# Row sums of the last four heads in one pass behind the attention, other pairs for the accumulating DMAs, and one load on GpSimd's queue

## The chip, the cores and the metric

The kernel runs on one core of one Trainium2 chip, alone. The metric is the device time of one execution in microseconds (us); lower is better. The core has a matrix engine (TensorE, PE in the profile), a vector engine (VectorE, DVE), an activation engine (ScalarE, ACT), GpSimd (POOL) and SyncE (SP). Each runs its own instructions strictly in order and waits for the others by semaphores. In this kernel SP and POOL mostly issue DMA transfers; the transfers of both run on the same 16 DMA engines. SP's transfers are queue q1 in the profile, POOL's are queue q0.

## What is computed

A gated mix of a 32-head attention block and a product-key expert layer over 2048 tokens of width 1024, all in float32:

```python
def _A_ref(x, wqkv, wo):                       # 32 heads of 32, 2048 tokens
    qkv = (x @ wqkv).reshape(B, S, 3, H, Dh).transpose(2, 0, 3, 1, 4)
    q, k, v = qkv[0], qkv[1], qkv[2]
    p = _softmax(jnp.einsum("bhqd,bhkd->bhqk", q, k) * (Dh ** -0.5), axis=-1)
    o = jnp.einsum("bhqk,bhkd->bhqd", p, v)
    return o.transpose(0, 2, 1, 3).reshape(B, S, D) @ wo
...
g = _sigmoid((x * gate_w).sum(-1, keepdims=True))
return g * _A_ref(x, A_wqkv, A_wo) + (1 - g) * b      # b: the expert layer
```

What matters here is the denominator of the softmax. The kernel computes the unnormalised output of a head and, apart from it, the sum of the exponentials of each query (the row sum); the factor gate / row sum is multiplied in only when the heads' outputs enter the last product with `wo`.

## The kernel before

Three stages follow each other. The first (up to about 480 us, and overlapping work to about 634 us) projects queries, keys and values and evaluates the expert layer. The second is the attention, head by head. The third multiplies the heads' outputs by `wo` in eight chunks of 256 tokens.

**Attention.** A head has 16 key tiles `kt` of 128 keys. For each, TensorE computes four score blocks of 512 queries into a ring of seven PSUM banks (`scores`, L1292), ScalarE takes their exponential into an SBUF tile `P[h, kt]` of 128 keys x 2048 queries (L1301), and TensorE multiplies the tile with the values (`pv`, L1313). The tile is also needed for the row sum: VectorE adds tiles to an accumulator `ACC[h]` (`presum` and `add`, L1354; one addition is two instructions of 128x1024). To relieve VectorE, some tiles are first added in pairs by an accumulating DMA from GpSimd's queue (`accumulate`, L1343: `P[h, b] += P[h, a]`), and only the sum is added to `ACC[h]` (`add_pair`, `merge`). `pairs_of` names the pairs (b, a). A place of a `P` tile is used again once its readers are done; `p_tile` picks the place by an estimate, `until`.

**Row sums.** For heads 0 to 27 the 128 partitions of `ACC[h]` are then folded to 32 by accumulating DMAs (`fold`, L1371), written to DRAM (`store_rows`, `SED`), folded there (`fold_rows`), and read back four heads together as `rr` (`load_r`), where VectorE adds the last two rows, takes the reciprocal and multiplies by the gate (`norm_r`); the result `RD` is the table of factors. The last four heads go another way. Head 29's accumulator is merged into the lower half of head 28's (`merge_odd`, `fold_odd`), and TensorE sums heads 28 and 29 with one product by a matrix of ones (`head_sums`, `rowsum`, L1326), head 30 with another; both use a bank of the ring within head 31's scores, which ScalarE empties (L1397). Head 31 is summed behind the attention, into a bank of its own. Each result goes to DRAM (`SMD`) by `norm_sums`, is read back by `load_r(7)`, and ends in `RD`.

**Order.** The order of work is written out by hand. A step is one key tile of one head (`base = 16 h`); `at(step, f, ...)` puts work to a step, and the main loop emits scores, the products with the values, the work of the step, then the addition of its tile. An engine's queue has its instructions in the order in which they are emitted.

**The last stage.** Chunk n needs the heads' outputs `OC[n]` (tile V, DRAM tensor `od`), the factors `RB[n]` (read from `RD`, tensor `rd`, each row copied to 32 partitions by the DMA), and their product split in a high and a low part (`split_o`, `scale_o` L1625, `split` L100 and L101). Chunks 0 and 1 are plain products (`wo_mm`, L1572); chunks 2 to 7 use a Strassen scheme of seven products P1 to P7 (`Halves.product`, L155), with prepared sums of `wo` (T1 to T4, DRAM tensors t0 to t3) loaded late. `RB[0]` is the tile `rb0`, which also serves as the accumulator of every third head; `RB[1]` and `RB[3]` share the place P9. `load_chunk(n)` loads `OC[n]` and `RB[n]`. Every DMA of SP waits for the eighth before it, since eight semaphores go round.

Of the kernel before, what the change touches and what calls it, by code (L numbers as in the profile page):

```python
# [10 lines left out]
F32 = mybir.dt.float32  # L11
# [6 lines left out]
S = 2048  # L18
# [14 lines left out]
def gated_mha_peer_kernel(ctx, tc, xT, wqkv, wv, wo, wq, k12, ug, v, out):  # L33
# [36 lines left out]

    ones2 = const.tile([128, 32], F32, name="ones2")
    nc.vector.memset(ones2, 0.0)
    for i in range(2):
        nc.vector.memset(ones2[64 * i:64 * i + 64, 16 * i:16 * i + 16], 1.0)


    const.tile([128, 152], F32, name="fill")
    ctx.enter_context(tc.tile_pool(name="fillr", bufs=1, side="right")).tile([128, 120], F32, name="fillr")
# [1083 lines left out]
    def p_tile(h, kt):  # L1162


        k = h * NT + kt
        n = [places for places, k0 in PLACES if k >= k0][-1]
        free = [i for i in range(n) if i not in (8, 9) or k < H * NT - 8]
        if k >= H * NT - 6:
            free = [i for i in free if i in ((0, 3, 7) if k >= H * NT - 2 else (1, 2, 3, 4, 5, 6))]
        i = min(free, key=lambda i: until[i])  # L1170
        pairs = pairs_of(h)
        until[i] = k + (16 if kt in [b for b, _ in pairs] else 10 if kt in [a for _, a in pairs] else 5)
        pool, name = ((pools["right"], f"P{i}") if i < 4 else (pools["left"], f"P{i}") if i < 8 else
                      (wk, f"P{i}") if i < 10 else (keep, ("vhl", "wo_raw2", "wo_raw3")[i - 10]))
        P[h, kt] = pool.tile([128, S], F32, name=name, bufs=1)
        return P[h, kt]
# [145 lines left out]

    def rowsum(ps, *srcs, ones=ones):
        for src in srcs:
            for qc in range(NQ):
                yield nc.tensor.matmul(ps[32 * qc:32 * qc + 32, :], ones,  # L1326
                                       src[:, qc * 512:(qc + 1) * 512],
                                       start=(src is srcs[0]), stop=(src is srcs[-1]))

# [30 lines left out]

    def merge_odd(h):
        add(ACC[h][up], ACC[h][up], pair(h, -1)[up])
        add(ACC[h - 1][low], ACC[h][low], pair(h, -1)[low])

    def fold_odd(h):
        nc.gpsimd.dma_start(ACC[h - 1][low], ACC.pop(h)[up], accum_op=OP.add)

    def fold(h, n):  # L1370
# [9 lines left out]

    def head_sums(h, heads=1):
        i, = ring_banks(1)
        for ins in rowsum(ring[:, i, :], ACC.pop(h), ones={1: ones, 2: ones2}[heads]):
            on_ring(ins, i)
        on_ring(norm_sums(h, ring[:, i, :], heads), i)

# [6 lines left out]

    def norm_sums(h, ps, heads=1):
        g, j = divmod(h, 4)
        o = wk.tile([128, 512], F32, name="ssb")
        ins = nc.scalar.activation(o, ps, AF.Copy)  # L1397
        for i in range(heads):
            dma(SMD[g][j + i:j + i + 1, :].rearrange("o (q s) -> (o q) s", q=NQ), o[32 // heads * i::32, :])
        return ins  # L1400

# [27 lines left out]
    def load_rb(n, k0, k1, js=range(4), queue=nc.sync):  # L1429
        if k0 == 0 and js[0] == 0:  # L1430
# [10 lines left out]

    OH, OL, W0 = {}, {}, []

    def split_first(step):
        o = OC[0][:, 0, :]
        if step == 0:
            W0.append(zp.tile([128, 2, D], F32R, name="z1"))
            OH[0] = zp.tile([128, KC, W], F32R, name="z0")
            OL[0] = wk.tile([128, KC, W], F32R, name="acc")
            nc.vector.tensor_mul(o, o, RB[0][:, 0, :])  # L1450
        elif step == 1:
            nc.scalar.activation(W0[0][:, 0], raw_wo(0), AF.Copy)
        elif step == 2:
            nc.scalar.activation(OH[0][:, 0, :], o, AF.Copy)
        else:
            for lo, src, hi in ((W0[0][:, 1], raw_wo(0), W0[0][:, 0]),
                                (OL[0][:, 0, :], o, OH[0][:, 0, :])):
                nc.vector.tensor_tensor(out=lo, in0=src, in1=hi.bitcast(F32), op=OP.subtract)
# [6 lines left out]
    for h in range(H):  # L1465
# [6 lines left out]
        if h < H - 1:  # L1472
# [16 lines left out]
        if j == 3 and g + 1 < G:  # L1489
# [77 lines left out]
    def wo_mm(pa, n, kcs, first, last):  # L1567
        for kc in kcs:
            wh, wl = (W0[0][:, 0], W0[0][:, 1]) if n == kc == 0 else (woh[kc], wol[kc])
            for a, b, i in ((OH[n], wh, 0), (OH[n], wl, 1), (OL[n], wh, 2)):  # L1570
                for tt, half in pa:
                    nc.tensor.matmul(pa[tt, half], a[:, kc, tt * 128:(tt + 1) * 128],  # L1572
                                     b[:, half * 512:(half + 1) * 512],
# [86 lines left out]
    for kc in range(1, KC - 1):  # L1660
        split_hi(kc + 1)
        if kc == 1:
            norm_sums(H - 1, sm)
            load_r(G - 1)
            pso.close()
# [165 lines left out]
```

## Time and profile before

| | us |
|---|---|
| median of three runs | 1808.73 |
| lowest and highest of them | 1805.19, 1809.46 |
| the profiled execution, its own time | 1804.75 |
| its span, first to last instruction | 1803.0 |
| TensorE busy in the span | 1795.0 |
| VectorE busy | 1495.4 |
| ScalarE busy | 1217.9 |
| GpSimd busy | 275.4 |
| SP's DMA queue, share of 16 engines | 36.4% |
| GpSimd's DMA queue, share of 16 engines | 36.4% |

The profiled execution is 4.0 us shorter than the median and 0.4 us shorter than the lowest run. Times within the trace count from the span's start. In the rows of a timeline the columns are start, duration, engine, line, operation, output and inputs by tile names, the shape and the number of merged instructions; a bracket tells the idle time before it and what ended it. Rows on SPq are the sequencer of SP while it issues a transfer. A matrix product in float32 appears as two instructions.

### The profile page before, as it was taken

How to read it: one execution, taken by the hardware profiler on the slowest of the kernel's cores; microseconds unless marked ns; L12 is line 12 of the kernel's file. 1: busy time of each engine (PE TensorE's matmuls, PEld its weight loads, DVE VectorE, ACT ScalarE, POOL GpSimd, SP SyncE). 2: the span in 40 equal slices, each digit the busy share in tenths (PEclk: the TensorE clock that was granted, in tenths of full speed). 3: DMA queues.
4: the chain of work that ended last, by engine and by line, in shares of the span. 5: the costliest groups of instructions: out<-in, count | busy, mean ns of one | idle time of the engine just before them, and what ended most of it. 6: DMA issues, size and time to landing. Idle time of an engine off the chain costs nothing.

```text
span 1803.0 us, 27887 instructions
## 1 busy us (share of the span) xinstructions
PE 1795.0 (100%) x10567; PEld 1136.7 (63%) x10567; DVE 1495.4 (83%) x1671; ACT 1217.9 (68%) x1608; POOL 275.4 (15%) x341
## 2 busy tenths in 40 slices
PE   9999999999999999999999999999999999999999
PEld 7877777788888855555554555555555545547787
DVE  7868776358987789999999999989989989895684
ACT  4434321211233399999999999999999999993221
POOL 0222000026401201111111111111111121111000
PEclk9999999999999999999999999999999999999999
DMA  6888888823238688899899999998999999977961
GB/s 237 242 284 249 276 264 288 269 79 107 83 119 283 229 197 170 179 182 204 174 206 195 195 205 191 193 196 192 201 221 197 202 220 193 201 161 204 280 179 66
DMA packets 132529, 361.14 MB, mean 200 GB/s; under 512 B 18516, under 2 KB 58596, under 8 KB 106968
## 3 DMA queue, kind: packets, MB, share of 16 engines
q0 software_dynamic: 22192, 132.79, 36.4%
q1 hardware_dynamic: 90040, 190.61, 36.4%
q10 hardware_dynamic: 20160, 35.92, 6.9%
q8 instruction: 84, 1.38, 0.3%
q14 instruction: 53, 0.43, 0.1%
HBM read 176.25 MB, written 86.09 MB: 146 GB/s over the span
## 4 chain that ended last, share of the span: by engine, by line
PE 96%; DMA 3%; SPq 1%; ACT 0%; DVE 0%; issue 0%; ACTq 0%; DVEq 0%
PE ring L1292 29%; PE o L1313 26%; PE bk L155 13%; PE bk L711 10%; PE pa L155 5%; PE bk L758 5%; PE bk L926 2%; PE bk L311 2%; PE bk L395 1%; PE bk L491 1%; SPq L82 1%; DMA wo_raw<-t1l 1%; DMA P<-rd 1%; PE pa L1579 1%; DMA smd<-ssb 0%; DMA woh<-t3h 0%
## 5 line engine op out<-in xcount | busy, mean ns | idle before, releaser
L1301 ACT ACTIVATE P<-ring 128x512 f32<-128x512 f32 (+3 forms) x982 | 807.3, 946 | 14.0 <-PE ring L1292 8.4
L1354 DVE TENSOR_TENSOR acc<-acc,P 128x1024 f32<-128x1024 f32 x418 | 482.2, 1218 | 26.5 <-ACT P L1301 26.5
L1313 PE MATMUL o<-P,V 128*32 128x512 f32 (+1 forms) x4040 | 414.4, 528 | 0.0
L1292 PE MATMUL ring<-Q,K 98*128 98x512 f32 x1024 | 269.0, 406 | 0.0
L1292 PE MATMUL ring<-z,z 98*128 98x512 f32 x1020 | 267.4, 406 | 0.1
L1292 PEld LDWEIGHTS ring<-Q,K 98*128 98x128 f32 x1024 | 182.8, 188 | 117.7 <-issue 37.0
L1292 PEld LDWEIGHTS ring<-z,z 98*128 98x128 f32 x1020 | 182.1, 188 | 114.7 <-ACT P L1301 38.9
L1313 PEld LDWEIGHTS o<-P,V 128*32 128x32 f32 x4040 | 111.5, 109 | 220.5 <-issue 200.5
L1354 DVE TENSOR_TENSOR rb<-rb,P 128x1024 f32<-128x1024 f32 (+1 forms) x188 | 217.4, 1218 | 11.6 <-ACT P L1301 11.6
L1343 POOL DMA_DIRECT2D P<-P x60 | 55.3, 922 | 427.5 <-PE o L1313 147.8
L240 ACT ACTIVATE hi<-bk 128x512 fp32r<-128x512 f32 x40 | 23.7, 595 | 118.5 <-PE bk L711 99.1
L1301 ACT ACTIVATE wo_raw<-ring 128x512 f32<-128x512 f32 (+3 forms) x110 | 99.4, 986 | 1.0 <-PE ring L1292 0.2
L711 PE MATMUL bk<-xh,e 128*128 128x512 f32 x384 | 94.2, 394 | 0.0
L711 PE MATMUL bk<-xl,e 128*128 128x512 f32 x384 | 92.3, 389 | 0.0
L711 PEld LDWEIGHTS bk<-xh,e 128*128 128x128 f32 x384 | 71.0, 188 | 22.0 <-issue 3.4
L253 DVE TENSOR_TENSOR lo<-bk,hi 128x512 fp32r<-128x512 f32 x40 | 27.6, 689 | 68.9 <-ACT hi L240 63.4
L711 PEld LDWEIGHTS bk<-xl,e 128*128 128x128 f32 x384 | 72.1, 188 | 15.0
L1301 ACT ACTIVATE vhl<-ring 128x512 f32<-128x512 f32 (+3 forms) x100 | 79.6, 881 | 0.9 <-PE ring L1292 0.6
L101 DVE TENSOR_TENSOR e<-wraw,e 128x512 fp32r<-128x512 f32 (+3 forms) x64 | 54.5, 859 | 26.6 <-ACT e L100 25.7
L100 ACT ACTIVATE e<-wraw 128x512 fp32r<-128x512 f32 (+3 forms) x64 | 44.7, 705 | 35.8 <-DMA wraw<-in_wqkv 20.2
L155 PE MATMUL bk<-xh,e 128*128 128x512 f32 x288 | 68.5, 393 | 0.0
L155 PE MATMUL pa<-woh,acc 128*128 128x512 f32 x192 | 62.6, 390 | 1.9 <-ACT acc L100 1.6
(311 smaller groups left out, 2445.0 us busy)
## 6 DMA issues: line engine op xcount, KB each, us to landing
P<-P POOLq DMA_DIRECT2D x60, 1024.0 KB, 10.5
wqt<-in_wq SPq DMA_DIRECT2D x26, 1024.0 KB
wraw<-in_wqkv SPq DMA_DIRECT2D x30, 512.0 KB
acc<-acc POOLq DMA_DIRECT2D x20, 512.0 KB, 5.5
qdh<-hi ACTq DMA_DIRECT2D x32, 256.0 KB
qdl<-lo ACTq DMA_DIRECT2D x32, 256.0 KB
kdh<-hi ACTq DMA_DIRECT2D x32, 256.0 KB
kdl<-lo ACTq DMA_DIRECT2D x32, 256.0 KB
```

Source lines behind the costliest of these rows:

```text
L100: nc.scalar.activation(hi, src, AF.Copy)
L101: (on or nc.vector).tensor_tensor(out=lo, in0=src, in1=hi.bitcast(F32), op=OP.subtract)
L155: nc.tensor.matmul(ps, self.a[a][i][:, k, :], self.b[b][j][k], start=(not first and k == 0 and i == j == 0), stop=(k == HC - 1 and i == 1))
L311: nc.tensor.matmul(ps[32 * quad:32 * quad + 32, :], kpad[:, quad % 2, i, :], t[:, quad, :], start=(i == 0), stop=(i == 3))
L711: nc.tensor.matmul(ps, t[:, kc // HC, a, kc % HC], x_at(b, n, kc), start=first, stop=last)
L758: nc.tensor.matmul(ps, x_at(a, t // 4, kc)[:, tok], b, start=first, stop=last)
L926: nc.tensor.matmul(p, x_at(a, t // 4, kc)[:, tok], b, start=first, stop=last)
L1292: on_ring(nc.tensor.matmul(ring[:, i, :], K[:98, kt * 128:(kt + 1) * 128], Q[:98, qc * 512:(qc + 1) * 512], start=True, stop=True), i)
L1301: on_ring(nc.scalar.activation(P[h, kt][:, q0 * 512:(q0 + m) * 512].rearrange("p (a m) -> p a m", a=m), ring[:, i:i + m, :], AF.Exp, scale ...
L1313: nc.tensor.matmul(O[h][32 * qc:32 * qc + 32, c0:c1], Vt[g][:, kt, 32 * j:32 * j + 32], p[:, qc * 512 + c0:qc * 512 + c1], start=(kt == 0) ...
L1343: nc.gpsimd.dma_start(P[h, b], P[h, a], accum_op=OP.add)
L1354: nc.vector.tensor_add(out[:, c], a[:, c], b[:, c])
```

## The change

Four things are changed together.

The row sums of heads 28 to 31 are all taken in one pass behind the attention. Heads 28 and 29 are now folded to 32 rows and stored like the others (into a new `SED[7]`); `merge_odd`, `fold_odd` and `head_sums` are gone. Head 30's accumulator is folded to 64 rows, and the stored 32 rows of heads 28 and 29 are read back into its other 64 partitions (`rows_back`, two transfers on GpSimd's queue). `rowsums` multiplies the two last tiles of head 31, its accumulator and this combined accumulator by columns of ones that put each head into 8 of 32 rows (`ones4`), into one bank. `norm_sums` writes four rows by four transfers.

The pairs become (0, 2), (3, 5), (6, 8) where they were (0, 2), (4, 6), (8, 10), and (0, 2), (6, 8) where they were (0, 2), (8, 10). Head 29 has two pairs in place of three. The estimate `until` of a pair's first tile is 18 steps in place of 16.

Since `rb0` is head 29's accumulator until its rows are stored, the factors of the first eight rows of chunk 0 go to a tile of their own (`load_first`, `zero`), those of 1 to 5 are loaded at step 11 of head 31, and `OL[0]` is made after the row sums.

The factors of chunk 3 (`load_rb(3)`) are loaded on GpSimd's queue, ahead of chunk 0's stores. Before, they followed `OC[3]` on SP's queue.

```diff
-    SED = [dram.tile([32, 4, S], F32, name=f"sed{g}") for g in range(G - 1)]
+    SED = [dram.tile([32, 4, S], F32, name=f"sed{g}") for g in range(G)]
...
+    ones4 = const.tile([128, 2, 32], F32, name="ones4")
+    nc.vector.memset(ones4, 0.0)
+    for rows, i, k in ((slice(64, 96), 0, 0), (slice(96, 128), 0, 1), (slice(0, 64), 0, 2), (slice(0, 128), 1, 3)):
+        nc.vector.memset(ones4[rows, i, 8 * k:8 * k + 8], 1.0)
...
-        if (h % 2 or (h % 4 and h < 17)) and h < 26 or h == H - 4:
-            return (0, 2), (8, 10)
-        return (0, 2), (4, 6), (8, 10)
+        if (h % 2 or (h % 4 and h < 17)) and h < 26 or h in (H - 4, H - 3):
+            return (0, 2), (6, 8)
+        return (0, 2), (3, 5), (6, 8)
...
-        until[i] = k + (16 if kt in [b for b, _ in pairs] else 10 if kt in [a for _, a in pairs] else 5)
+        until[i] = k + (18 if kt in [b for b, _ in pairs] else 10 if kt in [a for _, a in pairs] else 5)
...
+    def rowsums(ps, *srcs):
+        for k, (src, i) in enumerate(srcs):
             for qc in range(NQ):
+                nc.tensor.matmul(ps[32 * qc:32 * qc + 32, :], ones4[:, i], src[:, qc * 512:(qc + 1) * 512],
+                                 start=(k == 0), stop=(k == len(srcs) - 1))
...
+    def rows_back():
+        for j in range(2):
+            nc.gpsimd.dma_start(ACC[H - 2][64 + 32 * j:96 + 32 * j], SED[G - 1][:, j, :])
...
+    def norm_sums(ps):
         o = wk.tile([128, 512], F32, name="ssb")
+        nc.scalar.activation(o, ps, AF.Copy)
+        for j in range(4):
+            dma(SMD[G - 1][j:j + 1, :].rearrange("o (q s) -> (o q) s", q=NQ), o[8 * j::32, :])
...
+    def load_first():
+        zero["r"] = wk.tile([128, 512], F32, name="ssb")[:, :W]
+        for j in range(4):
+            dma(zero["r"][32 * j:32 * j + 32, :], RD[0, j:j + 1, :W].to_broadcast([32, W]))
...
-            at(base + NT + 6, merge_odd if h == H - 3 else merge, h)
-            if h == H - 2:
-                at(base + NT + 9, head_sums, h)
-            elif h == H - 3:
-                at(base + NT + 8, fold_odd, h)
-                at(base + NT + 15, head_sums, h - 1, 2)
-            else:
-                at(base + NT + 8, fold, h, 64)
-                if g + 1 < G:
-                    at(base + 2 * NT, fold, h, 32)
-                    at(base + 2 * NT + 8, store_rows, h)
+            at(base + NT + 6, merge, h)
+            at(base + NT + 8, fold, h, 64)
+            if h < H - 2:
+                at(base + 2 * NT, fold, h, 32)
+                at(base + 2 * NT + (5 if h == H - 3 else 8), store_rows, h)
...
-    at(30 * NT + 15, load_rb, 0, 0, KC - 2, range(2))
-    at((H - 1) * NT + 2, load_rb, 0, 0, KC - 2, range(2, 4))
-    at((H - 1) * NT + 13, load_rb, 0, KC - 2, KC - 1)
+    at(30 * NT + 15, load_first)
+    at((H - 1) * NT + 11, load_rb, 0, 1, KC - 2)
+    at((H - 1) * NT + 14, load_rb, 0, KC - 2, KC - 1)
+    at((H - 1) * NT + 14, rows_back)
...
-    list(rowsum(sm, *(P[H - 1, NT - i] for i in (1, 2)), ACC.pop(H - 1)))
+    rowsums(sm, *((P[H - 1, NT - i], 1) for i in (1, 2)), (ACC.pop(H - 1), 1), (ACC.pop(H - 2), 0))
+    OL[0] = wk.tile([128, KC, W], F32R, name="acc")
...
     split_o(1, HC, KC)
+    load_rb(3, 0, KC, queue=nc.gpsimd)
     load_at(2)
...
     plain_out(0, pa, nc.gpsimd)
-    load_chunk(3, 0, KC)
+    load_o(3, 0, KC)
```

On TensorE the order of scores and value products is the same as before; what is gone or moved are the products with ones. Before, the first of two such groups stood between the products with the values (tile V, bank `o`) and head 31's scores, in the ring:

```order
L1313 MATMUL o<-P_12566,V 32x512 x4
L1313 MATMUL o<-P_12573,V 32x256 x4
L1326 MATMUL ring<-acc,ones_111 32x512 x4
L1292 MATMUL ring<-Q_5229,K_5228 128x512 x9
L1313 MATMUL o<-P_12573,V 32x256 x4
```

Behind the attention, between the products of chunk 0's first eight rows (`pa`, inputs z and the low part) and those of its next, stood before:

```order
L1572 MATMUL pa_12927<-z_12763,acc 128x512
L1572 MATMUL pa_12928<-z_12763,acc 128x512
L1326 MATMUL o<-P_12878,ones 32x512 x4
L1326 MATMUL o<-P_12851,ones 32x512 x4
L1326 MATMUL o<-acc,ones 32x512 x4
L1572 MATMUL pa_12925<-woh_12909,z_12764 128x512
```

And stands in the change:

```order
L1559 MATMUL pa_12924<-z_12762,ssb 128x512
L1559 MATMUL pa_12925<-z_12762,ssb 128x512
L1326 MATMUL o<-P_12872,ones_112 32x512 x4
L1326 MATMUL o<-P_12847,ones_112 32x512 x4
L1326 MATMUL o<-acc,ones_112 32x512 x8
L1559 MATMUL pa_12922<-woh_12906,z_12763 128x512
```

Two groups of four products have left the ring, and one group of four has joined those behind the attention.

On GpSimd's queue, the end of the attention before (`acc<-rb` is `fold_odd`, P<-P are the pairs, `sed<-sed` folds in DRAM, `rr<-sed` the load of heads 24 to 27):

```order
L1366 DMA acc<-rb_5211 64x2048
L1343 DMA P_12443<-P_12480 128x2048
L1343 DMA P_12515<-P_12543 128x2048
L1378 DMA sed_94<-sed_94 16x1024
L82 DMA rr<-sed_94 128x2x64
L1343 DMA P_12655<-P_12688 128x2048
L1343 DMA P_12655<-P_12725 128x2048
```

And in the change (`rb<-rb` and `acc<-acc` are folds in SBUF, `sed_95` the new `SED[7]`):

```order
L1368 DMA sed_94<-sed_94 16x1024
L1361 DMA rb_5214<-rb_5214 32x2048
L82 DMA rr<-sed_94 128x2x64
L1365 DMA sed_95<-rb_5214 32x2048
L1342 DMA P_12653<-P_12687 128x2048
L1342 DMA P_12653<-P_12722 128x2048
L1361 DMA acc<-acc 64x2048
L1373 DMA acc<-sed_95 32x2048 x2
```

Head 30's fold and the two transfers of `rows_back` (L1373) stand behind the last pair of head 31; chunk 1's loads follow in both. In the same queue chunk 3's factors, four transfers of 32x8x256, now stand between chunk 1's loads and chunk 0's stores.

On VectorE, the first additions of head 30 before, with the numbers of the tiles (`rb0_5211` is head 29's accumulator; the 64x1024 rows are `merge_odd`):

```order
L1354 TENSOR_TENSOR acc_12461<-P1_12409,P8_12439 128x1024 x2
L1354 TENSOR_TENSOR acc_12461<-acc_12461,P7_12469 128x1024 x2
L1354 TENSOR_TENSOR rb0_5211<-rb0_5211,P0_12273 64x1024 x2
L1354 TENSOR_TENSOR acc_11984<-rb0_5211,P0_12273 64x1024 x2
L1354 TENSOR_TENSOR acc_12461<-acc_12461,P5_12504 128x1024 x2
L1354 TENSOR_TENSOR acc_12461<-acc_12461,P1_12518 128x1024 x2
```

And in the change:

```order
L1353 TENSOR_TENSOR acc_12497<-P9_12413,P0_12450 128x1024 x2
L1353 TENSOR_TENSOR rb0_5214<-rb0_5214,P1_12244 128x1024 x2
L1353 TENSOR_TENSOR acc_12497<-acc_12497,P2_12505 128x1024 x2
L1353 TENSOR_TENSOR acc_12497<-acc_12497,P9_12519 128x1024 x2
L1353 TENSOR_TENSOR acc_12497<-acc_12497,P1_12545 128x1024 x2
```

Before, the rows add tiles 1 and 3, tile 5, head 29's pair in two halves, then tiles 7 and 9. Now they add tiles 1 and 4, head 29's pair in one, then tiles 7, 9 and 10. From tile 9 on there are 21 additions (42 instructions) to the end of head 31 now; before, there were as many from tile 7 on.

More of the change, by code (lines that the diff above doesn't have):

```diff
@@ L69, in gated_mha_peer_kernel @@
     cbits = const.tile([1, 1], F32, name="cbits")
[L71 to L77, printed above, removed]
+    ones4 = const.tile([128, 2, 32], F32, name="ones4")
+    nc.vector.memset(ones4, 0.0)
+    for rows, i, k in ((slice(64, 96), 0, 0), (slice(96, 128), 0, 1), (slice(0, 64), 0, 2), (slice(0, 128), 1, 3)):
+        nc.vector.memset(ones4[rows, i, 8 * k:8 * k + 8], 1.0)
+    const.tile([128, 120], F32, name="fill")
     ctx.enter_context(tc.tile_pool(name="fillr", bufs=1, side="right")).tile([128, 120], F32, name="fillr")
@@ L1359, in gated_mha_peer_kernel @@
     up, low = slice(0, 64), slice(64, 128)
[L1361 to L1366, printed above, removed]
     def fold(h, n):
@@ L1379, in fold_rows @@
                              max_dma_last_dim=4 * S)
[L1381 to L1385, printed above, removed]
+    def rows_back():
+        for j in range(2):
+            nc.gpsimd.dma_start(ACC[H - 2][64 + 32 * j:96 + 32 * j], SED[G - 1][:, j, :])
     def finish(h):
@@ L1429, in load_rb @@
     def load_rb(n, k0, k1, js=range(4), queue=nc.sync):
-        if k0 == 0 and js[0] == 0:
+        if n not in RB:
             RB[n] = rb0 if n == 0 else wk.tile([128, KC, W], F32, name=f"P{8 + n % 2}", bufs=1)
@@ L1448, in split_first @@
             OH[0] = zp.tile([128, KC, W], F32R, name="z0")
-            OL[0] = wk.tile([128, KC, W], F32R, name="acc")
-            nc.vector.tensor_mul(o, o, RB[0][:, 0, :])
+            zero["lo"] = wk.tile([128, 512], F32R, name="ssb")[:, :W]
+            nc.vector.tensor_mul(o, o, zero["r"])
         elif step == 1:
@@ L1569, in wo_mm @@
             wh, wl = (W0[0][:, 0], W0[0][:, 1]) if n == kc == 0 else (woh[kc], wol[kc])
-            for a, b, i in ((OH[n], wh, 0), (OH[n], wl, 1), (OL[n], wh, 2)):
+            o_lo = zero["lo"] if n == kc == 0 else OL[n][:, kc]
+            for a, b, i in ((OH[n][:, kc], wh, 0), (OH[n][:, kc], wl, 1), (o_lo, wh, 2)):
                 for tt, half in pa:
-                    nc.tensor.matmul(pa[tt, half], a[:, kc, tt * 128:(tt + 1) * 128],
+                    nc.tensor.matmul(pa[tt, half], a[:, tt * 128:(tt + 1) * 128],
                                      b[:, half * 512:(half + 1) * 512],
@@ L1662, in gated_mha_peer_kernel @@
         if kc == 1:
-            norm_sums(H - 1, sm)
+            norm_sums(sm)
             load_r(G - 1)
```

15 lines of the change are left out of this document (2 added, 13 removed).

## Prediction

> **What bounds the kernel now.** I read the page's busy times first, then busy time by stretch, TensorE's waits in the last stage, and the timelines of the engines around the edits. A change of 0.3% (5.4 us) is about what a measurement of this kernel can tell from none.
>
> ```profile
> span 1803.0 us, 27887 instructions
> PE 1795.0 (100%) x10567; PEld 1136.7 (63%) x10567; DVE 1495.4 (83%) x1671; ACT 1217.9 (68%) x1608; POOL 275.4 (15%) x341
> ```
>
> TensorE is idle for 8.0 us of the span. By stretches (columns: start and end, length, busy time and instructions of PE, PEld, DVE, ACT, POOL, then TensorE's granted clock, DMA share, GB/s), the attention, the last stage and one head:
>
> ```profile
> 480.00:1618.00 1138.00, 1137.95 (x7535) 620.76 (x7537) 1042.89 (x996) 1031.72 (x1315) 172.49 (x227) 1.00 0.88 197
> 1618.00:1803.00 185.00, 179.32 (x816) 143.56 (x808) 115.07 (x165) 45.40 (x73) 9.52 (x17) 1.00 0.63 180
> 1036.91:1067.88 30.97, 30.97 (x217) 15.69 (x218) 29.68 (x27) 30.59 (x39) 4.77 (x8) 1.00 0.91 193
> ...
> PE pa L155 <- ACT acc L100: 1.6, 1, 1.6
> PE pa L155 <- DVE acc L101: 0.3, 1, 0.3
> ```
>
> The first two rows show TensorE without a gap in the attention and idle for 5.7 us behind it, of which the last two rows (TensorE's waits) are 1.86; the rest is the tail behind the last product. So this kernel has few microseconds to win: products that vanish, and 1.86. It has much to lose: in a head ScalarE is busy 30.59 and VectorE 29.68 of 30.97 us. One step, a key tile, is 30.97 / 16 = 1.94 us.
>
> **The products with ones.** TensorE around the two groups that are removed, and behind the attention:
>
> ```profile
> 1581.00 2.35 PE L1292 MATMUL ring<-z,z 98*128 98x512 f32 x9
> 1585.03 1.04 PE L1326 MATMUL ring<-acc,ones 128*32 128x512 f32 x8
> 1586.00 2.85 PE L1292 MATMUL ring<-Q,K 98*128 98x512 f32 x9
> 1606.83 1.04 PE L1326 MATMUL ring<-acc,ones 128*32 128x512 f32 x8
> ...
> 1625.74 1.04 PE L1326 MATMUL o<-acc,ones 128*32 128x512 f32 x8
> 1626.71 1.19 PE L1572 MATMUL pa<-woh,z 128*128 128x512 f32 x4
> ```
>
> A group costs 0.97 (1585.03 to 1586.00), two 1.94; the nine scores behind the first took 0.50 more than nine others (2.85 against 2.35). One group of 0.97 is added behind the attention, for the combined accumulator. So TensorE would reach its end 1.94 + 0.50 - 0.97 = 1.47 earlier, if nothing else held it.
>
> **VectorE holds it.** Its additions at the end of head 30 and in head 31:
>
> ```profile
> 1566.36 2.36 DVE L1354 TENSOR_TENSOR acc<-acc,P 128x1024 f32<-128x1024 f32 x2 [1.25 <-ACT P L1301]
> 1573.41 18.26 DVE L1354 TENSOR_TENSOR acc<-acc,P 128x1024 f32<-128x1024 f32 x16
> ...
> 1599.04 4.63 DVE L1354 TENSOR_TENSOR acc<-acc,P 128x1024 f32<-128x1024 f32 x4 [0.56 <-ACT P L1301]
> ...
> 1615.46 9.16 DVE L1354 TENSOR_TENSOR acc<-acc,P 128x1024 f32<-128x1024 f32 x8
> 1624.54 0.75 DVE L1599 TENSOR_TENSOR V<-V,rb 128x256 f32<-128x256 f32 x2
> ```
>
> From 1573.41 to the last addition, 1624.54, it does 21 additions (42 instructions) without a gap but 0.56: it is behind its tiles and would not feel TensorE running ahead. The last product with ones needs that addition: 1625.74 is 1.20 behind it. With the pairs (3, 5), (6, 8), head 30's unpaired tiles after its fifth step are 7 and 9 to 15, so the same 21 additions begin with tile 9. Tile 5 was ready at 1566.36; tile 9 is so four steps later, 1566.36 + 4 x 1.94 = 1574.1. The additions end at 1574.1 + 51.13 - 0.56 = 1624.7, 0.2 later than before. Behind them come head 31's accumulator and now one group more (0.97 each): chunk 0's products resume between 1626.7 and 1627.05, against 1626.71. The 1.47 is eaten by a wait that did not exist: **+0.3**, or -1.1 if the additions end 1.4 earlier.
>
> **The rows' way back.** The combined accumulator waits for two transfers on GpSimd's queue, behind the second pair of head 31 and the fold of head 30.
>
> ```profile
> 1609.13 0.85 POOL L1343 DMA_DIRECT2D P<-P  x1 [9.62 <-ACT z L1454]
> ...
> P<-P POOLq DMA_DIRECT2D x60, 1024.0 KB, 10.5
> acc<-acc POOLq DMA_DIRECT2D x20, 512.0 KB, 5.5
> ```
>
> Issue at 1609.13 + 0.85, landing within 10.5, some of the fold's 5.5 beside it, then some 5 to 6 for the read: it lands between 1622 and 1625, and is wanted at 1625.7. I take 0; if it is hidden no longer, each us is one of TensorE's, up to 5.
>
> **Four stores of row sums for one.** SP issues each in 0.53, and waits for the landing:
>
> ```profile
> 1586.76 1.06 SPq L82 DMA_DIRECT2D smd<-ssb  x2
> ...
> SPq L82 <- DMA smd<-ssb: 6.6, 1, 6.6
> ```
>
> Three more are 1.6 on the chain from row sums to factors. Chunk 0 and 1 run on 44 us of products (1626.71 to 1671.33) and only their last head groups need these factors; I take 0 here, with 1.6 as the other bound. Chunk 2 has about 1 to spare (next part), but its transfers are overtaken there by something larger.
>
> **Chunk 3's factors on the other queue.** Before, and the stall they cause:
>
> ```profile
> 1676.58 2.88 SPq L82 DMA_DIRECT2D P<-rd  x4
> ...
> 1688.75 2.36 DVE L1625 TENSOR_TENSOR V<-V,P 128x1024 f32<-128x1024 f32 x2 [7.78 <-DMA P<-rd]
> ...
> 1690.74 0.50 PE L155 MATMUL pa<-woh,acc 128*128 128x512 f32 x1 [1.57 <-ACT acc L100]
> ...
> DMA packets 1071, 1.04 MB, mean 115 GB/s; under 512 B 61, under 2 KB 1070, under 8 KB 1071
> q1 hardware_dynamic: 1071, 1.04, 88.7%
> ```
>
> Four issues from 1676.58 land just before 1688.75; VectorE waits 7.78 for them, and TensorE the 1.86 of above. The last two rows are the DMA view of 1678 to 1687: the load is 1 MB and holds 88.7% of all 16 engines for 9 us at only 115 GB/s, so 8.0 us of all engines. Moving it frees **1.86** there. Where does it go? Its place P9 is free once chunk 1's second half is multiplied:
>
> ```profile
> 1652.61 1.23 DVE L1640 TENSOR_TENSOR V<-V,P 128x1024 f32<-128x1024 f32 x1 [1.22 <-DMA P<-rd]
> 1652.80 10.58 SPq L82 DMA_DIRECT2D V<-od  x8
> ...
> 1664.34 1.23 DVE L1625 TENSOR_TENSOR V<-V,P 128x1024 f32<-128x1024 f32 x1 [4.89 <-DMA V<-od]
> 1668.43 1.23 DVE L1625 TENSOR_TENSOR V<-V,P 128x1024 f32<-128x1024 f32 x1 [2.87 <-DMA V<-od]
> 1669.58 0.69 DVE L101 TENSOR_TENSOR acc<-V,acc 128x512 fp32r<-128x512 f32 x1
> ...
> 1671.33 0.39 PE L155 MATMUL pa<-woh,acc 128*128 128x512 f32 x1
> ...
> 1650.00:1658.00 8.00, 8.00 (x37) 6.61 (x36) 3.31 (x4) 1.48 (x2) 0.00 (x0) 1.00 0.46 107
> 1658.00:1668.00 10.00, 10.00 (x46) 8.29 (x45) 2.52 (x3) 1.72 (x3) 2.15 (x4) 1.00 1.02 289
> ```
>
> P9 is free at 1652.61 + 1.23 = 1653.8, so the load is issued at about 1656 and moves from about 1658. There the DMA share is 1.02: these are the transfers of chunk 2 (`V<-od`, `P<-rd`) and the T sums, and VectorE waits for them already (4.89 and 2.87). The second half is multiplied at 1668.43, the low part of the first block is done at 1669.58 + 0.69 = 1670.27, and TensorE starts chunk 2 at 1671.33: 1.06 to spare. Eight us of engine time put into ten full ones must delay something by eight. If the queues take turns, SP's last transfer of chunk 2 ends about 8 later; I let 1 of it go to a share that falls to GpSimd only after 1668, so 7 later, and the stall is 7 - 1.06 = **6.0**. From below: with SP's transfers always first, the shift is some 0.5 and hidden. From above: if SP's queue stands while the load moves, the whole 9 and the 1.9 of start, less the spare, about 9.
>
> How two queues share can be seen once. From 1629 to 1636 GpSimd's queue reads factors the same way:
>
> ```profile
> q0 software_dynamic: 283, 0.82, 88.2%
> q1 hardware_dynamic: 19, 0.03, 1.0%
> ...
> 1634.69 0.33 SPq L82 DMA_DIRECT2D rr<-smd  x1
> ```
>
> SP's queue got 1.0% there, and the next SP issue came only at 1634.69, after the 6.6 of wait quoted above for a transfer of 8 KB. That leans away from "SP first" and toward a long delay; I stay between, since in that stretch SP had little to send.
>
> The Trainium skill ("Trainium Kernel Development and Optimization", Key Constraints) says that transfers issued from SP, ScalarE and GpSimd run on the same 16 DMA engines, and that several issuing engines save issue time alone. By that rule the move does not make 1 MB cheaper, only earlier, against full engines; the share of 1.02 agrees. "DMA: Bandwidth & Descriptors" (Queues, rings and completion order) says that an engine takes turns between queues packet by packet; by that rule alone the sum would be near its 6.0, but GpSimd's packets were larger in the rows above (0.82 MB in 283, some 2.9 KB, against 1 KB on SP's), which would give it more than half.
>
> **The pairs.** Each head has as many additions as before; in head 29 the pair that is gone costs one, and the merge that was done in two halves and is now one saves it. What could go wrong is a pair that is not there when its sum is added, or a `P` place that stays taken. A pair is issued four steps behind its first tile (steps 4, 7, 10), and the sums are added at steps 14, 18 and 22: 10, 11 and 12 steps later, 10 each before; 10 steps are 19.4 us, against the 10.5 of a pair. TensorE waits nowhere between 480 and 1618 now. I take 0; a missed place would cost some 2 per head (one step), over 31 heads up to 60, which I hold unlikely enough to leave it outside the range.
>
> **Sum.** +0.3 + 6.0 - 1.86 = +4.4 on the profiled execution's own time, 1804.75 (span 1803.0): 1809.2. The median of the runs is 1808.73, 3.98 above that execution; I carry the difference over to the median: 1813.2, 0.25% slower.
>
> **The rivals.**
> 1. *The move is hidden* (SP's transfers are not pushed back). For it: SP's transfers are issued from 1652.80, before the load. Against it: shares of 1.02 and 1.0%. Then 1.86 is won and VectorE takes 0.3 to 0.5 back: -1.4 to -1.6; with the 1.47 of TensorE's too, -3.3. Time 1805.4 to 1807.3: not slower, the other side of my forecast. It decides if the delay is below 1.06 + 1.86.
> 2. *SP's queue stands for the whole load.* For it: the 1.0%. Against it: P<-rd and V<-od of chunk 2 are partly through by 1658. Stall 9: +7.4, 1816.2. It decides from a stall of about 7 on.
> 3. *The rows come back late.* For it: only 1 to 3 us of room, in a queue of transfers of 10.5. Against it: little else moves then. Up to 5 on top of the forecast: +4.4 to +9.4, 1813 to 1818.
>
> **Chances.** Forecast 0.45 (its own range +2 to +6.5, 1810.7 to 1815.2), first rival 0.25, second 0.15, third 0.15. Range 1804 to 1820: the first rival's best with a spread of the median (1805.19 to 1809.46) to the third's worst. Faster by over 0.3% needs more than 5.4, which the removable work (1.47 + 1.86) does not hold: 0.06. Slower by over 0.3%: second rival 0.15, most of the third 0.10, the upper part of the forecast 0.19: 0.44. The rest, 0.50, is within.
>
> **What would show it.** At 1671 or some us later TensorE waits for chunk 2's first high or low part, with 5 to 7 of idle time, and DVE's scale_o(2) waits longer for V<-od; nothing near 1690. If TensorE starts chunk 2 without a wait, the first rival stands. The last addition of head 31 ends at 1624.5 to 1625.1, and TensorE waits there for it; a release by a DMA is the third rival. A head in the middle takes 30.97 still. A longer head would prove me wrong about the pairs, and the end of additions before 1623.5 about VectorE.

## The result and the profile after

| | before | after |
|---|---|---|
| median of six runs | 1806.45 us | 1813.49 us |
| lowest and highest | 1804.27 to 1809.46 | 1812.95 to 1816.45 |
| ratio of times, 95% interval | | 1.0040 (1.0027 to 1.0053) |
| span of the profiled execution | 1803.0 us | 1812.2 us |

The changed kernel is 0.40% slower, some 7 us. (The median of before was 1808.73 when the prediction was made; three more runs moved it.)

The page of the changed kernel (span, busy times), TensorE's waits from the end of the attention on, and busy time by stretch, with the columns of the prediction:

```profile
span 1812.2 us, 27968 instructions
...
PE 1798.1 (99%) x10559; PEld 1136.5 (63%) x10559; DVE 1495.0 (82%) x1673; ACT 1216.4 (67%) x1604; POOL 281.6 (16%) x351
```

```profile
PE pa L155 <- ACT acc L100: 4.7, 1, 4.7
PE o L1326 <- DMA acc<-sed: 2.1, 1, 2.1
PE pa L155 <- DVE acc L101: 0.2, 1, 0.2
```

```profile
480.00:1618.00 1138.00, 1137.89 (x7532) 621.22 (x7534) 1041.96 (x996) 1031.22 (x1312) 175.14 (x231) 1.00 0.88 196
...
1626.00:1630.00 4.00, 1.91 (x12) 0.21 (x12) 3.92 (x7) 1.67 (x3) 1.56 (x4) 1.00 0.95 300
1630.00:1634.00 4.00, 4.00 (x14) 3.16 (x11) 2.68 (x6) 3.81 (x6) 2.52 (x5) 0.57 1.01 330
1676.00:1681.00 5.00, 0.36 (x2) 0.00 (x0) 1.76 (x2) 0.58 (x1) 0.00 (x0) 1.00 1.04 399
1681.00:1684.00 3.00, 2.71 (x6) 1.70 (x7) 2.30 (x4) 0.68 (x2) 0.00 (x0) 0.55 1.02 428
```

The attention is as full as before. There are two waits behind it, one of 2.1 for the rows that come back, one of 4.9 at chunk 2; the 1.9 at chunk 3 is gone. And TensorE is busy for 3.1 us more, though it has eight matrix instructions fewer: behind each of the two waits its granted clock is near half (0.57, 0.55). TensorE's timeline shows the same; the last number of a row's head is the duration:

```profile
1582.32 2.35 PE L1292 MATMUL ring<-z,z 98*128 98x512 f32 x9
...
1624.88 2.07 PE L1326 MATMUL o<-acc,ones 128*32 128x512 f32 x8
1629.05 1.06 PE L1326 MATMUL o<-acc,ones 128*32 128x512 f32 x8 [2.09 <-DMA acc<-sed]
1630.05 2.05 PE L1559 MATMUL pa<-woh,z 128*128 128x512 f32 x4
1631.90 1.84 PE L1559 MATMUL pa<-wol,z 128*128 128x512 f32 x4
1633.57 1.08 PE L1559 MATMUL pa<-woh,acc 128*128 128x512 f32 x4
...
1675.29 1.07 PE L1559 MATMUL pa<-woh,acc 128*128 128x512 f32 x4
1681.10 0.64 PE L155 MATMUL pa<-woh,acc 128*128 128x512 f32 x1 [4.74 <-ACT acc L100]
...
1685.85 0.40 PE L155 MATMUL pa<-z,s 128*128 128x512 f32 x1
```

Against the rows of before, where the span's 9.2 us come from:

- 1.3 lie ahead of the edits to the last heads: the same scores of head 30 stand at 1582.32, 1581.00 before. 1.2 of it is there at the attention's first exponentials already (629.31 against 628.11), ahead of all pairs. Stage one ends earlier or later in each execution (in the profiles of the experiments below these exponentials stand between 0.5 earlier and 1.1 later than those of before), so I don't count this as an effect of the change.
- Chunk 0 goes on at 1630.05 in place of 1626.71, 3.34 later; without the 1.3 that is about the wait of 2.09.
- Its next eight instructions, 1630.05 to 1633.57, take 3.5 in place of 1.96 (1626.71 to 1628.67): 1.6.
- The wait at chunk 2 is 4.74 + 0.18 = 4.9, and the first product, 1681.10 to 1685.85, takes 4.75 in place of 2.72 (1671.33 to 1674.05), of which 1.85 are slow products.
- Chunk 3 saves its 1.86 and about 0.4 of slower products behind it.

1.3 + 2.1 + 1.6 + 4.9 + 1.85 - 2.3 = 9.45; the 0.25 over are not followed further.

### The profile page after: what moved, and what is told of

It is laid out like the page before. It is cut to its first block, busy times and chain, and to the rows that moved or that the text cites. A ratio compares the mean times of both kernels' runs of the same rounds, so it can differ in the third digit from the quotient of the medians.

```text
span 1812.2 us, 27968 instructions
## 1 busy us (share of the span) xinstructions
PE 1798.1 (99%) x10559; PEld 1136.5 (63%) x10559; DVE 1495.0 (82%) x1673; ACT 1216.4 (67%) x1604; POOL 281.6 (16%) x351
## 4 chain that ended last, share of the span: by engine, by line
PE 90%; DMA 4%; ACT 2%; DVE 1%; SPq 1%; issue 1%; POOL 0%; ACTq 0%; DVEq 0%; POOLq 0%
PE ring L1292 27%; PE o L1313 25%; PE bk L155 11%; PE bk L711 9%; PE pa L155 6%; PE bk L758 5%; PE bk L926 2%; PE bk L311 2%; PE bk L491 1%; ACT P L1301 1%; SPq L82 1%; DMA wraw<-in_wqkv 1%; DMA V<-od 1%; PE bk L395 1%; PE pa L1566 1%
## 5 line engine op out<-in xcount | busy, mean ns | idle before, releaser
L1353 DVE TENSOR_TENSOR acc<-acc,P 128x1024 f32<-128x1024 f32 x408 | 469.4, 1215 | 22.1 <-ACT P L1301 22.1
L1353 DVE TENSOR_TENSOR rb<-rb,P 128x1024 f32<-128x1024 f32 x186 | 214.3, 1215 | 5.6 <-ACT P L1301 5.6
L1342 POOL DMA_DIRECT2D P<-P x60 | 55.7, 928 | 362.9 <-PE o L1313 141.8
L1353 DVE TENSOR_TENSOR acc<-acc,wo_raw 128x1024 f32<-128x1024 f32 x60 | 70.1, 1216 | 1.8 <-ACT wo_raw L1301 1.8
```

The lines of the kernel that those rows point to most:

```text
L1342: nc.gpsimd.dma_start(P[h, b], P[h, a], accum_op=OP.add)
L1353: nc.vector.tensor_add(out[:, c], a[:, c], b[:, c])
```

## The experiments

All ratios are to the kernel before, measured beside each experiment, with 95% intervals. Its median differed from one time to another (1805.74 to 1806.65), so the rows are compared by their ratios.

| kernel | median us | ratio |
|---|---|---|
| the change | 1813.49 | 1.0040 (1.0027 to 1.0053) |
| e1_sp | 1810.53 | 1.0022 (1.0013 to 1.0032) |
| e2_fold | 1810.15 | 1.0022 (1.0012 to 1.0031) |
| e3_both | 1807.74 | 1.0007 (0.9997 to 1.0017) |
| e4_pool | 1810.28 | 1.0022 (1.0013 to 1.0032) |
| e5_fill | 1813.34 | 1.0040 (1.0026 to 1.0055) |
| e6_pairs | 1808.73 | 1.0012 (1.0002 to 1.0021) |
| e7_halves | 1804.38 | 0.9994 (0.9985 to 1.0004) |
| e8_step | 1805.62 | 0.9995 (0.9985 to 1.0004) |
| e9_clock | 1811.70 | 1.0033 (1.0021 to 1.0045) |
| e10_swap | 1805.96 | 1.0000 (0.9991 to 1.0009) |
| e11_pairs | 1808.91 | 1.0017 (1.0008 to 1.0026) |
| e12_store | 1804.65 | 0.9992 (0.9983 to 1.0001) |

**The load back on SP's queue (e1_sp).**

```diff
-    load_rb(3, 0, KC, queue=nc.gpsimd)
...
-    load_o(3, 0, KC)
+    load_chunk(3, 0, KC)
```

> The changed kernel with chunk 3's factors back on SP's queue, behind OC[3], as before. Theory (the collision): the 4.74 + 0.18 us that TensorE waits at 1681 and the slow products behind it (1681.10 to 1685.85 in place of 2.72, 2.0 us) go, and the wait of 1.9 at the start of chunk 3 comes back with 0.7 of slow products: 1813.5 - 6.9 + 2.6 = about 1809. Rival (the wait comes from the later row sums and the four stores, not from the load): TensorE still waits 4 to 5 us at the start of chunk 2, about 1813 to 1816.

Its waits of TensorE behind the attention, and one stretch:

```profile
PE o L1326 <- DMA acc<-sed: 3.4, 1, 3.4
PE pa L155 <- DVE acc L101: 0.3, 1, 0.3
```

```profile
1630.00:1634.00 4.00, 4.00 (x13) 2.86 (x10) 1.92 (x4) 3.49 (x6) 2.17 (x4) 0.50 0.90 232
```

The wait at chunk 2 is gone, so the load was its cause, not the later row sums or the four stores, which are all still there. Against the change the ratio fell by 0.18%, about 3.2 us, less than the 4.3 expected: the wait for the rows stands, here with 3.4 and a clock of 0.50 behind it. The wait of 1.9 at chunk 3, expected back, isn't (0.3 is left): TensorE comes there later, and starts chunk 3 at 1694.70 in place of 1690.74.

**The load alone moved, in the kernel before (e4_pool).** The opposite edit.

> The kernel before with only chunk 3's factors moved to GpSimd's queue, at the same place as in the change. Theory (the collision alone): TensorE waits 5 to 6 us at the start of chunk 2 and runs about 2 us of slow products, and the 1.9 + 0.7 at chunk 3 goes: 1806.5 + 4.5 to 5.5 = 1811 to 1812. Rival (the move costs something only with the later row sums of the change): within 1.5 of 1806.5, or faster by up to 2.6.

```profile
1676.30 0.80 PE L155 MATMUL pa<-woh,acc 128*128 128x512 f32 x1 [4.37 <-ACT acc L100]
```

The same wait at the same place, 4.37 and 0.62 more before the third product. The move alone makes the kernel before 3.6 us slower; expected were 4.5 to 5.5.

How the transfers met is in the changed kernel's own trace: GpSimd's issues and VectorE's wait, SP's issue of chunk 2's other input, and the two queues' packets, MB and share of the 16 engines from 1661 to 1670, with the time from issue to landing:

```profile
1658.85 2.34 POOL L82 DMA_DIRECT2D P<-rd  x4 [24.51 <-DVE V L1627]
...
1657.84 13.37 SPq L82 DMA_DIRECT2D V<-od  x8
...
1679.16 2.54 DVE L1612 TENSOR_TENSOR V<-V,P 128x1024 f32<-128x1024 f32 x2 [14.84 <-DMA V<-od]
```

```profile
q1 hardware_dynamic: 801, 0.76, 57.5%
q0 software_dynamic: 189, 0.66, 33.2%
...
P<-rd POOLq DMA_DIRECT2D x1, 256.0 KB, 15.5
```

VectorE waits 14.84 for SP's `V<-od`, whose issue stretches to 13.37 (10.58 before). SP's queue does not stand still: it has 57.5% against 33.2%, and the load takes 15.5 for a quarter.

**Head 30's fold ahead of head 31's second pair (e2_fold).**

```diff
-            at(base + b + 4, accumulate, h, b, a)
+            at(base + (9 if (h, a) == (H - 1, 6) else b + 4), accumulate, h, b, a)
```

> The changed kernel with head 30's fold issued ahead of head 31's second pair on GpSimd's queue, nothing else. Theory (the fold waits on the queue behind a pair that waits for the first pair's landing): the rows are back some 4 us earlier, the 2.09 us of TensorE's wait for them and the 1.6 us of slow products behind it go, chunk 2's wait becomes up to 1.6 longer because its transfers start only 2 earlier: -2 to -3.7, about 1810 to 1811.5. Rival (the rows are late because SP's factor load holds the DMA engines from 1611 to 1624): the fold's place moves the landing by less than 1, the wait stays over 1 us, and the time within 1 of 1813.5.

GpSimd's issues (L1342 a pair, L1361 a fold, L1373 the rows coming back), in the changed kernel and then in this experiment:

```profile
1609.07 0.88 POOL L1342 DMA_DIRECT2D P<-P  x1 [9.56 <-ACT P L1301]
1609.62 1.18 POOL L1361 DMA_DIRECT2D acc<-acc  x1
1620.56 0.52 POOL L1373 DMA_DIRECT2D acc<-sed  x1 [9.77 <-DMA acc<-acc]
1622.47 0.51 POOL L1373 DMA_DIRECT2D acc<-sed  x1 [1.39 <-DMA rb<-rd]
```

```profile
1603.67 0.83 POOL L1361 DMA_DIRECT2D acc<-acc  x1 [5.70 <-DVE acc L1353]
1608.26 0.90 POOL L1342 DMA_DIRECT2D P<-P  x1 [3.75 <-ACT P L1301]
1609.73 0.52 POOL L1373 DMA_DIRECT2D acc<-sed  x1 [0.57 <-DMA acc<-acc]
```

In the change the fold is ready at about 1605 (VectorE's run of additions that it waits for ends at 1604.90), but is issued at 1609.62, behind a pair that waits. The row names ScalarE; but the first pair, whose sum goes into the same tile, was issued at 1598.61 and took 9.9 to land. Then the fold shares the engines with the second pair's megabyte and takes 10.7 to land (5.8 in the experiment); the read starts at 1620.56. What the two queues had of the engines in the change, from 1612 to 1620 and from 1620 to 1624:

```profile
q0 software_dynamic: 176, 1.18, 84.8%
q1 hardware_dynamic: 364, 0.25, 11.5%
```

```profile
q1 hardware_dynamic: 458, 0.41, 91.5%
q0 software_dynamic: 12, 0.07, 6.4%
```

So it is GpSimd's own queue, not SP's factor load, that fills the engines while the fold runs; SP's load does so when the read begins. In the experiment the read starts at 1609.73, and TensorE no longer waits for it (in its profile it waits 1.5 for an operand of chunk 0 instead, whose factors come late on SP's queue, and 4.0 at chunk 2). The rows land near 1625, 4 earlier as expected, though their read starts 10.8 earlier: its second transfer takes 13.4 to land in this profile, 6.7 at most in the change and 6.9 in e3_both. Why it took so long there was not followed. The ratio fell by 0.18% here too. So the order of two instructions on GpSimd's queue made the rows late, as the theory had it.

**Both edits (e3_both).**

> Both of these edits: the load back on SP's queue, and the fold ahead of the pair. Theory: what is left of the change are the row sums and the pairs, which I forecast at +0.3: 1805 to 1807, no different from before (1806.45). Rival (the pairs or the row sums cost something of their own): over 1808.5, with a wait of TensorE elsewhere.

1807.74 is just above the expected range, and not distinguishable from before. The row of VectorE behind its last addition, and TensorE's only waits of over 0.2:

```profile
1624.60 0.75 DVE L1586 TENSOR_TENSOR V<-V,rb 128x256 f32<-128x256 f32 x2
```

```profile
PE pa L155 <- ACT acc L100: 1.6, 1, 1.6
PE pa L155 <- DVE acc L101: 0.3, 1, 0.3
```

By the start of what stands behind them, the additions end at 1624.60 (1624.54 before), and the waits are those of the kernel before: the row sums and pairs together neither cost nor gain anything that can be told (the interval is -0.5 to +3 us).

**Products by zeros in the waits (e5_fill, e9_clock).** To learn whether the slow products come from the idle time, the waits are filled with products that add zero to the row sums, or go to a bank that nobody reads. e5_fill fills both waits of the change, e9_clock the one wait that e1_sp has left.

```diff
+    def idle_products(ps, src, rounds):
+        for i in range(4 * rounds):
+            qc = i % 4
+            nc.tensor.matmul(ps[32 * qc:32 * qc + 32, :], zeros, src[:, :512], start=False, stop=False)
...
     def rowsums(ps, *srcs):
         for k, (src, i) in enumerate(srcs):
+            if k == len(srcs) - 1:
+                idle_products(ps, srcs[0][0], 4)
```

This is e9_clock; e5_fill has two rounds here, and five before chunk 2.

> The changed kernel with products by a matrix of zeros (32 columns of ones' place, 0.97 us for four) in TensorE's two waits: two rounds of four between the sum of head 31's accumulator and that of the combined one, five rounds before chunk 2. They add zero to the row sums, or go to a bank that is not read. Theory (the products behind a wait are slow because TensorE's clock falls in the wait): the waits are filled to within 0.5, chunk 0's first products take 1.0 per four again in place of 2.05, chunk 2's first takes 0.4 in place of 0.64, granted clock 1.0 in 1628 to 1636 and over the start of chunk 2, and the time falls by 2.5 to 3.5: 1810 to 1811. Rival (the products are slow for another reason, such as DMA traffic into the same memory): they stay slow, the time stays within 1 of 1813.5.

> Experiment e1_sp (in which only the wait for the rows is left, 3.4 us in its profile, and nothing waits behind it before chunk 3) with four rounds of products by zeros in that wait, added to the row sums as zero. Theory (the wait costs a second time, by the clock): the sum of the combined accumulator takes 1.0 again in place of 1.9 and chunk 0's next twelve products 2.9 in place of 4.7, granted clock 1.0 from 1628 to 1636 in place of 0.5; 2 to 2.8 us less than e1_sp's 1810.5: 1807.7 to 1808.5. Rival (the clock falls whatever TensorE does there, or the products are slow for lack of data): no less than 1810.

The stretch behind the filled wait in e9_clock (0.50 in e1_sp, above), then its start of chunk 3 and that of e1_sp:

```profile
1630.00:1634.00 4.00, 4.00 (x18) 3.31 (x19) 2.42 (x4) 4.00 (x7) 1.12 (x2) 1.00 1.06 182
...
1694.37 0.50 PE L157 MATMUL pa<-woh,acc 128*128 128x512 f32 x1 [2.08 <-ACT acc L102]
```

```profile
1694.70 0.50 PE L155 MATMUL pa<-woh,acc 128*128 128x512 f32 x1
```

On the clock the theory holds: full speed, 18 instructions in the 4 us in place of 13. On the time it fails: 1811.70 against 1810.53, ratios that can't be told apart, where 2 to 2.8 less was expected. TensorE came earlier to chunk 3, where it waited 2.08 for chunk 3's factors and began at 1694.37; without the filling it began there at 1694.70, with no wait ahead of its first product. In e5_fill the slow products behind the first wait are gone likewise, though 1.10 of the wait was left. The wait at chunk 2, meant to be filled by 4.5 us of products, ended 2.22 us after them, the clock fell behind it all the same (0.54 from 1684.5 to 1688), and the time is that of the change.

**The pairs (e6_pairs, e11_pairs).** The new pairs in the kernel before; and the old pairs in e7_halves (below), whose row sums are those of the change.

```diff
-            return (0, 2), (8, 10)
-        return (0, 2), (4, 6), (8, 10)
+            return (0, 2), (6, 8)
+        return (0, 2), (3, 5), (6, 8)
...
-        until[i] = k + (16 if kt in [b for b, _ in pairs] else 10 if kt in [a for _, a in pairs] else 5)
+        until[i] = k + (18 if kt in [b for b, _ in pairs] else 10 if kt in [a for _, a in pairs] else 5)
```

> The kernel before with only the pairs (0, 2), (3, 5), (6, 8) and the estimate of 18 steps; head 29 keeps three pairs. Theory: no wait of TensorE in the attention, a head takes 30.97, the last additions end 0 to 0.5 later than 1624.5 relative to TensorE; time within 1.5 of the kernel before (1806.65). Rival (a pair or a place that is late): a wait of TensorE between 480 and 1618, over 1809.

> Experiment e7_halves with the pairs and the estimate of the kernel before ((0, 2), (4, 6), (8, 10); (0, 2), (8, 10); 16 steps), heads 28 and 29 with two pairs each. Theory (the pairs are worth nothing by themselves: VectorE's last stretch has the same 21 additions): the last addition within 0.4 of e7_halves relative to TensorE, time within 1 of 1804.4. Rival (the pairs were needed for a place of a P tile or an addition): a wait of ScalarE or TensorE in heads 30 or 31, 1806 or more.

ScalarE's row that waits, in e6_pairs and then in e11_pairs:

```profile
1618.31 3.83 ACT L1301 ACTIVATE P<-ring 128x512 f32<-128x512 f32 x5 [2.64 <-DVE acc L1354]
```

```profile
1561.65 0.60 ACT L1301 ACTIVATE P<-ring 128x512 f32<-128x512 f32 x1 [3.01 <-DVE rb L1353]
```

Both theories fall. Each waits once for a `P` place that VectorE has not read yet, and costs, by the ratios, about 2 us against before and 4 against e7_halves. TensorE waits 1.75 and 1.76 for it, and runs at half its clock for some 3.4 us soon after. So in these two runs the pairs and the row sums of the last four heads were not to be had one without the other. In e6_pairs head 29 keeps three pairs and in e11_pairs it has two, as the row sums go; which place goes to which tile is decided by `until`, and was not followed further.

**Toward a better version (e7_halves, e8_step, e10_swap, e12_store).** e7_halves is e3_both with chunk 3 loaded in halves:

```diff
-    load_chunk(3, 0, KC)
+    load_chunk(3, 0, HC)
+    load_chunk(3, HC, KC)
...
-                if name == "A11":
-                    scale_o(n + 1)
+                if name in ("A11", "S3"):
+                    scale_o(n + 1, [name == "S3"])
```

> Experiment e3_both with chunk 3 loaded in halves on SP's queue (four heads' groups of OC[3] and their factors, then the other four), and the first block's high and low part made after the first half. Theory (the wait of 1.9 at the start of chunk 3 is the end of one row of transfers, of which the first product needs only half): TensorE starts chunk 3 without a wait; a wait under 0.7 may stand before its second product; 2 us less than e3_both: 1805 to 1806. Rival (the second half is later, so that the second product waits as long as the first did): the same time as e3_both, 1807.7.

The wait at chunk 3 is gone; what is left:

```profile
PE pa L155 <- DVE rb L161: 1.0, 2, 0.6
```

Its ratio is 0.13% below that of e3_both, with intervals that overlap, and against the kernel before its interval still holds 1. e8_step moves `load_rb(0, 1, KC - 2)` from step 11 to 8, e10_swap sums the combined accumulator ahead of head 31's, e12_store puts chunk 1's stores on GpSimd's queue.

> The same with the factors of chunk 0's groups 1 to 5 loaded from step 8 of head 31 in place of step 11. Theory (these transfers, which hold the DMA engines from 1611 to 1624, end at the moment when their factors are wanted, so that in some executions chunk 0's second group waits for them): they land 4 to 6 earlier, the spread of the runs and the median fall by up to 1: 1804.5 to 1805.5. Rival (in order on SP's queue they wait for the store of head 29's rows, and hold up what stands behind them, the last factors' store among it): no gain, or a wait elsewhere, 1806 or more.

> Experiment e7_halves with the combined accumulator summed ahead of head 31's own. Theory (TensorE waits for VectorE's last addition, and by then the rows are back): the sum of the rows goes into that wait, chunk 0 goes on 0.8 to 0.9 earlier relative to the last addition, 1803.5 to 1804 against 1804.4. Rival (the rows come no earlier than the last addition, or chunk 0's next operands are not ready): the same or longer, 1804.4 or more.

> Experiment e7_halves with the four stores of chunk 1 on GpSimd's queue in place of SP's. Theory (what is left after e7_halves, two waits of TensorE of 1.0 in all for VectorE's sums at 1693 to 1697, comes from these stores, which stand behind chunk 3's loads on SP's queue, so that VectorE's next sums wait for their place): these waits go, 0.5 to 1.5 less than e7_halves: 1803 to 1804 where before is 1805.7 to 1806.7, a ratio of 0.9985 to 0.999. Rival (the stores take engine time from chunk 4's loads, or the waits have another cause): the same as e7_halves, a ratio of 0.9994 or more.

None of the three adds anything that can be told from e7_halves. In e10_swap chunk 0 went on at 1625.17, 1.12 behind the last addition (1.98 in e7_halves), as expected, and the time did not follow: in its profile the waits for VectorE's sums in the last stage are 2.5 (3.2 in e8_step's), where e7_halves has 1.0. e12_store's waits fell from 1.0 to 0.7:

```profile
PE pa L155 <- DVE rb L161: 0.4, 1, 0.4
PE pa L155 <- DMA wol<-t3l: 0.3, 1, 0.3
```

No version here is shown to beat the kernel before.

## Why the prediction was right, and where not

The time, 1813.49, lies beside the predicted 1813.2, but much of that is luck: the step forecast was +4.4, the measured one is +7.0, and the median of before came out 2.3 lower than the one that I added to. By its step, and by the sign that I had named for it (a release by a DMA), what came is not the forecast (+2 to +6.5) but the third rival, the late rows on top of the forecast's stall (+4.4 to +9.4), to which I gave 0.15. Slower by over 0.3% had 0.44, within it 0.50; the ratio 1.0040 is on the first side, with an interval that reaches to 1.0027.

- **What bounds it.** Right: little to win (the best versions, e7_halves and e12_store, stand 0.06% and 0.08% below before, within their intervals), and what is lost is TensorE waiting and, behind its waits, running slower.
- **The products with ones.** Right. TensorE reached the sum of head 31's accumulator at 1624.88, 0.86 earlier than before (1625.74) although it had started 1.3 later: 2.2 of the 2.44 that the two removed groups and the slow scores were worth.
- **VectorE holds it.** Right: the last addition was forecast at 1624.7, and ended at 1624.60 in e3_both; in the change at 1625.85, with the 1.3 of its later start. About 1.0 of the 1.47 went into the wait for it, which in the rows is hidden in the 2.07 of the group at 1624.88 (1.04 before). In e3_both, without the other waits, chunk 0 goes on at 1626.58, 0.1 earlier than before, where +0.3 was forecast.
- **The rows' way back.** The term of the sum that was mis-sized most. I took 0, landing between 1622 and 1625; they landed near 1629, and the wait was 2.1. The sum itself was wrong: 1609.98 + 10.5 + 6 is 1626.5, behind the 1625.7 at which the rows are wanted, with nothing yet for the fold. I had put the fold at 5.5, "beside" the second pair's 10.5; issued behind that pair, it took 10.7. The read, two transfers issued 1.9 apart, took 8.5 in all in place of 5 to 6. The reason that I gave against the third rival, that little else moves then, does not hold either: SP's queue had 91.5% of the engines from 1620 to 1624. e2_fold shows the order of fold and pair as the cause.
- **The four stores.** 0 was right as far as can be seen: with them in place, e1_sp and e3_both start chunk 2 without a wait.
- **Chunk 3's factors.** The mechanism was right, its size a little off: 4.9 for 6.0, and in e4_pool, where the rows are not late, 4.37 + 0.62 = 5.0. e1_sp and e4_pool show the load as cause from both sides. The 1.86 at chunk 3 is gone as forecast, but that the move won it is not shown: in e1_sp, with the load back on SP's queue, it is gone but for 0.3 too. GpSimd's larger packets (0.66 MB in 189, against 0.76 in 801) did not bring its queue more than half of the engines, as I had thought possible: it got 33.2%. The second rival (SP's queue stands) falls with SP's 57.5%, the first (the move is hidden) with the wait.
- **The pairs.** 0 was right within the change, but the reason, that pairs and places had room, was not the whole one: e6_pairs and e11_pairs show a place that is late as soon as the pairs and the row sums are not changed together.
- **Missing altogether.** The clock behind a wait: 1.6 and 1.85 of slower products in the profile, 3.4 in all, which is more than any other term was off. Without it the waits give 2.1 + 4.9 - 1.86 = 5.1 for the profile, whose span grew by 7.9 behind the 1.3 of its later start.

## What to carry to other kernels

Where the DMA engines are full, a load that is issued earlier on another queue doesn't get its own time; it takes that of the transfers which are wanted first, here 4.9 us lost for 1.9 won at the most. On an in-order queue the instruction to look at is the one behind a waiting one: two exchanged issues were worth about 3 us. And a microsecond saved on TensorE ahead of a stage that waits for transfers can come back as a wait in it, as in e9_clock: before counting a gain, find the next point whose end a transfer sets.

## What was not expected of the hardware

TensorE can pay for a wait twice. Behind the waits of 2.09 and 4.74 us (the change), 3.40 (e1_sp) and 4.37 (e4_pool) its granted clock was 0.50, for 3.4 us each time in the change and for some 6.8 in the other two; with the wait filled by products by zeros it was 1.00 (e9_clock). At half speed 3.4 us do the work of 1.7, and the slow products of the change cost 1.6 and 1.85.

The length of the wait alone does not decide it. Waits of 1.57 (before, chunk 3, where the first products were some tenths longer), 1.81 (e8_step) and 2.08 (e9_clock, chunk 3) left the clock at 1.00, and one of 1.75 (e6_pairs) halved it. Nor does the clock fall with the wait: in e2_fold a wait of 3.54 ends at 1676.14, and the clock is full until 1677.5. The stretches behind these waits, in e6_pairs, e9_clock and e2_fold (the clock is the third number from the end):

```profile
1618.96:1619.50 0.54, 0.54 (x5) 0.30 (x9) 0.54 (x2) 0.54 (x2) 0.00 (x0) 1.00 0.00 0
1619.50:1623.00 3.50, 3.50 (x20) 0.90 (x22) 3.50 (x4) 2.65 (x3) 0.00 (x0) 0.51 0.31 47
```

```profile
1694.37:1698.00 3.63, 3.34 (x13) 2.47 (x14) 2.85 (x5) 0.63 (x1) 0.00 (x0) 1.00 1.02 387
```

```profile
1676.10:1677.50 1.40, 0.87 (x3) 0.44 (x4) 1.40 (x3) 0.00 (x0) 0.00 (x0) 1.00 0.97 410
1677.50:1681.00 3.50, 3.50 (x9) 2.71 (x10) 2.10 (x4) 1.70 (x3) 0.00 (x0) 0.51 1.02 416
```

The Trainium skill ("TensorE: Matmul & The Clock Gate", What's actually happening) has a clock that is halved after an idle window of about 3.4 us and comes back after as long a busy one. The half and the 3.4 us agree; that waits of 1.75 and of 2.09 (with about 1 more hidden in the group ahead of it) were enough is less than the page's window. Why one of 2.08 was not is left open here.
